# Expert tiles rounded to 64 rows: 192-row tiles with a half-array tail, and two nests of conditional tiles

## Chip, cores, metric

One core of one Trainium2 chip. The metric is the device time of one execution in microseconds (us). Profiles come from single executions; the times that are compared come from several executions of both kernels on the same chip.

## The reference, cut to what matters

Chunked attention (4 batches, 8 heads, 768 positions, head size 64) gives 3072 rows of 512. Each row goes to one of 8 experts, or stays with the expert of the row before it:

```python
fresh_e = int(np.argmax(logits[b, s]))
e = fresh_e if s == 0 or local_gate[b, s] < 0.5 else prev_e
h = np.maximum(x[b, s] @ w1[e], 0.0)        # w1[e]: 512 x 1024
out[b, s] = p[e] * (h @ w2[e])              # w2[e]: 1024 x 512
```

Everything is float32. With the fixed inputs the experts get 561, 195, 431, 505, 757, 256, 96 and 271 rows.

## The kernel before

The rows are scattered to DRAM in the order of their experts, and the second half of the kernel walks over *tiles*: 128 rows of one expert, gathered by GpSimd. Every expert is rounded up to whole tiles. 24 tiles exist for any input ("sure"); up to 7 more are conditional, in nested branches on a count that the chip works out. "Hidden" is the first matmul with ReLU, "product" the second.

```python
def product(ht, w2_sb, xs, past):
    y_ps = yps.tile([P, D], F32, name="y_ps")
    for m in range(FK):
        nc.tensor.matmul(y_ps, lhsT=ht[:, m], rhs=w2_sb[:, m], start=(m == 0), stop=(m == FK - 1))
    # ... scale by the probability on ScalarE, then an indirect store by GpSimd

def maybe_tiles(ctx, xts):
    n_tiles = nc.values_load(n_i, ...)
    for j in range(NTILE - SURE):
        i = SURE - EARLY + j
        ctx.enter_context(tc.If(n_tiles > i))
        w1_sb, w2_sb = weights(late, i, wa)           # 4 MB, pool of two buffers
        ht = hidden(xts[j % 2], w1_sb)
        if j + 1 < NTILE - SURE:
            rows_turned(late, i + 1, rest[:, j + 1], xt=xts[(j + 1) % 2])   # transposes of the next tile
        product(ht, w2_sb, rest[:, j], late[2][:, i:i + 1])
# ... the loop over sure tiles: weights from three buffers (pools wa, wa, wb);
#     maybe_tiles stands before sure tile BRANCH = SURE - 4, whose weights wait in wb
```

## Time and profile before

| | us |
|---|---|
| timed, median of 3 | 516.05 |
| span of the profiled execution | 540.6 |
| of it, up to the first product | 147.5 |
| of it, first product to the end of the last ("tile stage") | 386.9 |
| one tile, hidden to hidden | 14.45 |

The profiled execution was 25 us slower than the timed ones.

### The profile page before, as it was taken

The numbers are of one execution on the slowest core, as the hardware profiler recorded it, in microseconds if no ns is written. First come the engines' busy times: TensorE is split into PE (matmuls) and PEld (weight loads), VectorE is DVE, ScalarE is ACT, GpSimd is POOL, SyncE is SP. The second block draws the span as 40 slices with busy tenths as digits, with TensorE's granted clock in tenths as the row PEclk, the third lists the DMA queues.
The fourth block names the chain that finished last, engine by engine and source line by source line (L and its number), as shares of the span: only waits on it lengthen the run. The fifth ranks groups of instructions, "written<-read, shape, count | busy, mean of one in ns | idle before, by whom it ended". The sixth has DMA issues, their size and how long they took to land. (4 is left out here: it accounts for less than half of the span.)

```text
span 540.6 us, 9452 instructions
## 1 busy us (share of the span) xinstructions
PE 517.5 (96%) x3604; PEld 395.8 (73%) x3604; DVE 103.0 (19%) x394; ACT 112.5 (21%) x234; POOL 95.8 (18%) x141
## 2 busy tenths in 40 slices
PE   8997897889899999999999999999999999999995
PEld 6997786788776777777777777777777677777772
DVE  2464555635433000000000000000000100000000
ACT  4564445332211111011111110111011011111110
POOL 2002211530333211111111222221110100010000
PEclk9999989956999999999999999999999999999998
DMA  8977767896999998998989899999999985069700
GB/s 303 380 251 230 219 201 224 267 399 271 326 341 312 388 342 333 342 330 313 332 317 325 329 336 337 348 328 356 349 341 326 341 303 212 21 257 413 306 21 19
DMA packets 52760, 157.98 MB, mean 292 GB/s; under 512 B 7707, under 2 KB 11805, under 8 KB 52704
## 3 DMA queue, kind: packets, MB, share of 16 engines
q1 hardware_dynamic: 45696, 135.96, 70.5%
q0 software_dynamic: 6720, 20.78, 10.3%
q8 instruction: 32, 0.52, 0.4%
q10 hardware_dynamic: 288, 0.52, 0.3%
q14 instruction: 24, 0.20, 0.1%
HBM read 144.62 MB, written 13.40 MB: 292 GB/s over the span
## 5 line engine op out<-in xcount | busy, mean ns | idle before, releaser
L754 PE MATMUL y_ps<-w_sb,ht 128*128 128x512 f32 x416 | 183.0, 592 | 0.0
L743 PEld LDWEIGHTS h_ps<-gxt,w_sb 128*128 128x128 f32 x1408 | 160.7, 192 | 10.1 <-issue 10.1
L743 PE MATMUL h_ps<-gxt,w_sb 128*128 128x128 f32 x1408 | 161.3, 275 | 0.0
L754 PEld LDWEIGHTS y_ps<-w_sb,ht 128*128 128x128 f32 x416 | 76.9, 190 | 86.6 <-issue 85.9
L759 POOL DMA_INDIRECT out_dram<-y,to x27 | 27.3, 1010 | 235.6 <-ACT y L758 192.3
L681 DVE COPY gxt<-g_ps 128x512 f32<-128x512 f32 x22 | 15.2, 692 | 273.4 <-PE g_ps L678 269.7
L746 ACT ACTIVATE ht<-h_ps 128x512 f32<-128x512 f32 x54 | 32.2, 597 | 154.0 <-PE h_ps L743 105.2
L615 PE MATMUL o_ps<-vt,pt 128*96 128x65 f32 x512 | 57.2, 268 | 6.3 <-issue 6.2
L615 PEld LDWEIGHTS o_ps<-vt,pt 128*96 128x96 f32 x512 | 53.3, 183 | 10.7 <-issue 8.0
L758 ACT ACTIVATE y<-y_ps,xs 128x512 f32<-128x512 f32 x24 | 16.5, 687 | 161.8 <-PE y_ps L754 149.3
L463 POOL DMA_INDIRECT x_dram<-x,row x32 | 29.6, 925 | 102.9 <-DVE lt L385 66.2
L615 PEld LDWEIGHTS s_ps<-qt,kt 64*128 64x128 f32 x512 | 31.5, 196 | 6.6 <-issue 4.6
L615 PE MATMUL s_ps<-qt,kt 64*128 64x96 f32 x512 | 34.6, 286 | 0.6 <-ACT pt L345 0.4
L345 ACT ACTIVATE pt<-s_ps,mask_mid 128x256 f32<-128x256 f32 x72 | 28.1, 482 | 22.6 <-remote 9.8
L743 PE MATMUL h_ps<-held_xt,w_sb 128*128 128x128 f32 x256 | 29.3, 275 | 0.9 <-ACTq _compat.py:109 0.9
L743 PEld LDWEIGHTS h_ps<-held_xt,w_sb 128*128 128x128 f32 x256 | 28.9, 192 | 1.7 <-ACTq _compat.py:109 1.7
L355 DVE TENSOR_TENSOR x<-o_ps,rinvs 96x256 f32<-96x256 f32 x64 | 26.2, 417 | 1.2
L363 ACT COPY xt<-xt_ps 128x384 f32<-128x384 f32 x32 | 15.4, 482 | 42.1 <-PE xt_ps L615 32.4
L574 POOL DMA_INDIRECT xs<-x_dram,rows_late x19 | 18.3, 963 | 11.2 <-DMA x_dram<-x,row 5.7
L354 DVE RECIPROCAL rinvs<-o_ps 96x4 f32<-96x4 f32 x64 | 10.7, 172 | 48.0 <-PE o_ps L615 42.3
L615 PE MATMUL xt_ps<-ident,x 96*128 96x96 f32 x128 | 18.2, 270 | 0.5 <-ACT xt L363 0.5
L756 POOL TENSOR_TENSOR to<-xs,past_late 128x1 int32<-128x1 int32 x19 | 3.5, 187 | 77.4 <-DMA out_dram<-y,to 72.8
(163 smaller groups left out, 218.7 us busy)
## 6 DMA issues: line engine op xcount, KB each, us to landing
w_sb<-in_w_dram SPq DMA_DIRECT2D x216, 512.0 KB
vt<-in_v_dram SPq DMA_DIRECT2D x32, 260.0 KB
kt<-in_k_dram SPq DMA_DIRECT2D x30, 256.0 KB
qt<-in_q_dram SPq DMA_DIRECT2D x32, 192.0 KB
kt<-in_k_dram ACTq DMA_DIRECT2D x2, 256.0 KB
x_dram<-x,row POOLq DMA_INDIRECT x32, 6.0
out_dram<-y,to POOLq DMA_INDIRECT x27, 8.0
xs<-x_dram,rows_late POOLq DMA_INDIRECT x19, 6.6
```

The lines of the kernel that those rows point to most:

```text
L345: nc.scalar.activation(pt[:, :, :, c], st[:, :, :, c], ACT.Exp, bias=m[:, g:g + 1], scale=SCALE)
L355: nc.vector.tensor_tensor(x[:, 0:D].rearrange("p (a u d) -> p u a d", u=2, d=DH)[:, u], o_ps[:, :, 0:DH], rinv.to_broadcast([QB, HP, DH]), ...
L363: nc.scalar.copy(xt, xt_ps)
L463: ins = nc.gpsimd.indirect_dma_start(out=x_dram[:, :], out_offset=bass.IndirectOffsetOnAxis(ap=row[:, n:n + 1], axis=0), in_=x[0:QB, j + n ...
L574: ins = nc.gpsimd.indirect_dma_start(out=xs.bitcast(I32), out_offset=None, in_=x_dram[:, :], in_offset=bass.IndirectOffsetOnAxis(ap=rows[: ...
L615: return lambda *a, **k: tc.keep_in_program_order(f(*a, **k))
L681: nc.vector.tensor_copy(xt, g_ps)
L743: nc.tensor.matmul(h_ps[:, m], lhsT=w1_sb[:, kk, P * (g + m):P * (g + m) + P], rhs=xt[:, kk], start=(kk == 0), stop=(kk == DK - 1))
L746: nc.scalar.activation(ht[:, g:g + 4], h_ps, ACT.Relu)
L754: nc.tensor.matmul(y_ps, lhsT=ht[:, m], rhs=w2_sb[:, m], start=(m == 0), stop=(m == FK - 1))
L758: nc.scalar.activation(y, y_ps, ACT.Copy, scale=xs[:, D:D + 1])
L759: return nc.gpsimd.indirect_dma_start(out=out, out_offset=bass.IndirectOffsetOnAxis(ap=to, axis=0), in_=y, in_offset=None, bounds_check=NT ...
```

## The change

Its intent: to round experts up to 64 rows instead of 128. Where a rest of 64 would have cost a whole tile, a *wide* tile of 192 rows takes it along: hidden runs on 192 columns, and the last 64 rows' product puts the two halves of the output columns side by side on the two column halves of the array. There are now twelve sure tiles, a nest of up to 19 conditional ones, and a second nest of up to 8 wide ones. For these inputs 27 tiles become 5 early, 16 late and 3 wide.

```diff
-SURE = NT // P
-NTILE = SURE + E - 1
+UNIT = 64
+MORE = P + UNIT
+SURE = 12
+NTILE = 31
@@ plan_late
...
+        units = whole(total, "units", UNIT - 1, UNIT)
+        nc.vector.scalar_tensor_tensor(units, done, -2.0, units, ALU.mult, ALU.add)
+        pairs = whole(units, "pairs", 1, 2)
...
+        nc.vector.scalar_tensor_tensor(wide, pairs, 2.0, units, ALU.mult, ALU.is_gt)
+        nc.vector.scalar_tensor_tensor(wide, units, 2.0, wide, ALU.is_gt, ALU.mult)
...
+    def unit_product(ht, w2_sb, xs, past, y):
+        d = D // 2
+        y_ps = xps.tile([P, d], F32, name="yu_ps", tag="xps")
+        for m in range(FK):
+            for u in range(2):
+                h = slice(UNIT * u, UNIT * u + UNIT)
+                nc.tensor.matmul(y_ps[h], lhsT=ht[:, m, P:MORE], rhs=w2_sb[:, m, d * u:d * u + d],
+                                 start=(m == 0), stop=(m == FK - 1), tile_position=(0, UNIT * u))
...
+    def wide_tiles(ctx, n_wide):
+        for j in range(E):
+            ctx.enter_context(tc.If(n_wide > j))
+            if j + 1 < E:
+                wide_gathered(j + 1)
+            w1_sb, w2_sb = weights(wide, j, wa)
+            ht = hidden(wide_xt[j % 2], w1_sb, rows=MORE, ht=wide_ht[j % 2])
+            if j + 1 < E:
+                wide_turned(j + 1)
+            xs, xs_unit = wide_slots(j)
+            product(ht, w2_sb, xs, wide[2][:, j:j + 1])
+            unit_product(ht, w2_sb, xs_unit, unit[2][:, j:j + 1], wide_y[j % 2])
...
         if i == BRANCH:
-            maybe_tiles(held_xt[1:])
...
+            maybe_tiles(n_tiles)
+            wide_tiles(n_wide)
```

Left out: the gathers of conditional rows move into the first nest, two tiles ahead; for the wide tiles one tile ahead; the late plan gets two more parts.

More of the change, by code (lines that the diff above doesn't have):

```diff
@@ L42 @@
 BRANCH = SURE - 4
+RING = 4
 LOADS = 6
@@ L477, in totals, with plan @@
         return total
-    def plan(name, nt, sums):
+    def plan(name, nt, sums, unit=False):
         no = iota([P, nt, 1], [[1, nt], [0, 1]], 0, 0, f"no_{name}")
-        place = iota([P, nt, 1], [[P, nt], [0, 1]], 1, 1, f"place_{name}")
+        if unit:
+            place = one([P, nt, 1], F32, f"place_{name}")
+            for u in range(2):
+                nc.gpsimd.iota(place[UNIT * u:UNIT * u + UNIT], pattern=[[P, nt], [0, 1]], base=P + 1,
+                               channel_multiplier=1, allow_small_or_imprecise_dtypes=True)
+        else:
+            place = iota([P, nt, 1], [[P, nt], [0, 1]], 1, 1, f"place_{name}")
         table = one([1, nt], I32, f"table_{name}")
@@ L489, in all_tiles @@
             return a.rearrange("p (o e) -> p o e", o=1).to_broadcast([P, nt, n])
-        scratch = sm.tile([P, nt * PLAN], F32, name=f"scratch_{name}")
+        scratch = sm.tile([P, (NTILE - EARLY) * PLAN], F32, name="scratch")
         at, parts = 0, []
@@ L509, in plan @@
         nc.vector.tensor_tensor(is_past, place_at, last, op=ALU.is_gt)
-        nc.vector.tensor_scalar(past, is_past, float(FAR), None, ALU.mult)
+        if unit:
+            for u in range(2):
+                h = slice(UNIT * u, UNIT * u + UNIT)
+                nc.vector.tensor_scalar(past[h], is_past[h], 2.0 * FAR, float(u), ALU.mult, ALU.add)
+        else:
+            nc.vector.tensor_scalar(past, is_past, float(FAR), None, ALU.mult)
         nc.vector.tensor_tensor(place_at, place_at, last, op=ALU.min)
@@ L534, in plan_sums, with whole @@
         return sums
-    def tiles_of(total, name, more):
-        i = sm.tile([E, 1], I32, name=f"tiles_i_{name}")
-        nc.vector.tensor_scalar(i, total, float(more), None, ALU.add)
-        nc.vector.tensor_scalar(i, i, 7, None, ALU.logical_shift_right)
-        t = sm.tile([E, 1], F32, name=f"tiles_{name}")
+    def whole(a, name, more, size):
+        i = sm.tile([E, 1], I32, name=f"{name}_i")
+        nc.vector.tensor_scalar(i, a, float(more), None, ALU.add)
+        nc.vector.tensor_scalar(i, i, size.bit_length() - 1, None, ALU.logical_shift_right)
+        t = sm.tile([E, 1], F32, name=name)
         nc.vector.tensor_copy(t, i)
@@ L546, in plan_early @@
         total = totals("early", FORE)
-        full = tiles_of(total, "early", 0)
+        full = whole(total, "tiles_early", 0, P)
         yield
@@ L560, in plan_late @@
         total = totals("late", B)
-        tiles = tiles_of(total, "late", P - 1)
-        nc.vector.tensor_tensor(tiles, tiles, done, op=ALU.subtract)
-        sums = plan_sums("late", total, tiles, done)
-        n_i = once.tile([1, 1], I32, name="n_i")
-        nc.vector.tensor_copy(n_i, sums[0:1, E:E + 1])
-        return plan("late", NTILE - EARLY, sums), n_i
+        units = whole(total, "units", UNIT - 1, UNIT)
+        nc.vector.scalar_tensor_tensor(units, done, -2.0, units, ALU.mult, ALU.add)
+        pairs = whole(units, "pairs", 1, 2)
+        wide = one([E, 1], F32, "wide")
+        nc.vector.scalar_tensor_tensor(wide, pairs, 2.0, units, ALU.mult, ALU.is_gt)
+        nc.vector.scalar_tensor_tensor(wide, units, 2.0, wide, ALU.is_gt, ALU.mult)
+        tiles = one([E, 1], F32, "tiles_late")
+        nc.vector.scalar_tensor_tensor(tiles, wide, -2.0, pairs, ALU.mult, ALU.add)
+        before_wide = one([E, 1], F32, "before_wide")
+        nc.vector.tensor_tensor(before_wide, tiles, done, op=ALU.add)
+        n_i = once.tile([1, 2], I32, name="n_i")
+        sums = plan_sums("late", total, tiles, done)
+        nc.vector.tensor_copy(n_i[:, 0:1], sums[0:1, E:E + 1])
+        late = plan("late", NTILE - EARLY, sums)
+        sums = plan_sums("wide", total, wide, before_wide)
+        nc.vector.tensor_copy(n_i[:, 1:2], sums[0:1, E:E + 1])
+        return late, plan("wide", E, sums), plan("unit", E, sums, unit=True), n_i
     SP = mybir.EngineType.SP
@@ L680, in rows_turned, with unit_turned @@
             xt = hp.tile([P, DK, P], F32, name="gxt")
-        nc.vector.tensor_copy(xt, g_ps)
+        nc.vector.tensor_copy(xt[:, :, 0:P], g_ps)
         return xt, past[:, i:i + 1]
+    def unit_turned(xs, xt):
+        g_ps = xps.tile([P, DK, UNIT], F32, name="u_ps", tag="xps")
+        for kk in range(DK):
+            nc.tensor.transpose(g_ps[:, kk], xs[0:UNIT, P * kk:P * kk + P], identity=ident[:UNIT, :UNIT])
+        nc.vector.tensor_copy(xt[:, :, P:MORE], g_ps)
     def first_turned():
@@ L721, in everything @@
     flat = rinvs.rearrange("p n u a o -> p (n u a o)")
-    ok = sm.tile([P, (NTILE - EARLY) * PLAN], F32, name="scratch_late")[0:QB, 0:NB * H]
+    ok = sm.tile([P, (NTILE - EARLY) * PLAN], F32, name="scratch")[0:QB, 0:NB * H]
     nc.vector.tensor_scalar(ok, flat, 1.0 / SAFE, None, ALU.is_ge)
@@ L735, in everything, with hidden @@
     yps = ctx.enter_context(tc.tile_pool(name="yps", bufs=2, space=PSUM))
-    def hidden(xt, w1_sb, between={}):
-        ht = hp.tile([P, FK, P], F32, name="ht")
-        for g in range(0, FK, 4):
-            h_ps = hps.tile([P, 4, P], F32, name="h_ps")
-            for m in range(4):
+    def hidden(xt, w1_sb, between={}, rows=P, ht=None):
+        if ht is None:
+            ht = hp.tile([P, FK, P], F32, name="ht")
+        many = 512 // rows // 2 * 2
+        for g in range(0, FK, many):
+            h_ps = hps.tile([P, many, rows], F32, name="h_ps")
+            for m in range(many):
                 for kk in range(DK):
-                    nc.tensor.matmul(h_ps[:, m], lhsT=w1_sb[:, kk, P * (g + m):P * (g + m) + P], rhs=xt[:, kk],
-                                     start=(kk == 0), stop=(kk == DK - 1))
-                if m == 3:
-                    nc.scalar.activation(ht[:, g:g + 4], h_ps, ACT.Relu)
+                    nc.tensor.matmul(h_ps[:, m], lhsT=w1_sb[:, kk, P * (g + m):P * (g + m) + P],
+                                     rhs=xt[:, kk, 0:rows], start=(kk == 0), stop=(kk == DK - 1))
+                if m == many - 1:
+                    nc.scalar.activation(ht[:, g:g + many], h_ps, ACT.Relu)
                 for f in between.get(g + m, ()):
@@ L753, in product @@
         for m in range(FK):
-            nc.tensor.matmul(y_ps, lhsT=ht[:, m], rhs=w2_sb[:, m], start=(m == 0), stop=(m == FK - 1))
+            nc.tensor.matmul(y_ps, lhsT=ht[:, m, 0:P], rhs=w2_sb[:, m], start=(m == 0), stop=(m == FK - 1))
         to = hp.tile([P, 1], I32, name="to", bufs=4)
@@ L761, in product, with maybe_gathered, wide_slots, wide_gathered @@
             bounds_check=NT - 1, oob_is_err=False).ins
+    half_rows = out.rearrange("n (u d) -> (n u) d", u=2)
+    def unit_product(ht, w2_sb, xs, past, y):
+        d = D // 2
+        y_ps = xps.tile([P, d], F32, name="yu_ps", tag="xps")
+        for m in range(FK):
+            for u in range(2):
+                h = slice(UNIT * u, UNIT * u + UNIT)
+                nc.tensor.matmul(y_ps[h], lhsT=ht[:, m, P:MORE], rhs=w2_sb[:, m, d * u:d * u + d],
+                                 start=(m == 0), stop=(m == FK - 1), tile_position=(0, UNIT * u))
+        to = hp.tile([P, 1], I32, name="to", bufs=4)
+        token = xs[:, D + 1:XW].bitcast(I32)
+        nc.gpsimd.tensor_tensor(to, token, past, op=ALU.add)
+        nc.gpsimd.tensor_tensor(to, to, token, op=ALU.add)
+        nc.scalar.activation(y, y_ps, ACT.Copy, scale=xs[:, D:D + 1])
+        nc.gpsimd.indirect_dma_start(
+            out=half_rows, out_offset=bass.IndirectOffsetOnAxis(ap=to, axis=0), in_=y, in_offset=None,
+            bounds_check=2 * NT - 1, oob_is_err=False)
+    def maybe_gathered(j):
+        gathered(late, SURE - EARLY + j, range(B), rest[:, j % RING])
+    def wide_slots(j):
+        return rest[:, RING + 2 * (j % 2)], rest[:, RING + 2 * (j % 2) + 1]
+    def wide_gathered(j):
+        for t, xs in zip((wide, unit), wide_slots(j)):
+            gathered(t, j, range(B), xs)
+    def maybe_turned(j):
+        rows_turned(late, SURE - EARLY + j, rest[:, j % RING], xt=held_xt[1 + j % 2])
+    def wide_turned(j):
+        xs, xs_unit = wide_slots(j)
+        rows_turned(wide, j, xs, xt=wide_xt[j % 2])
+        unit_turned(xs_unit, wide_xt[j % 2])
     @with_exitstack
-    def maybe_tiles(ctx, xts):
-        n_tiles = nc.values_load(n_i, min_val=SURE - EARLY, max_val=NTILE - EARLY,
-                                 skip_runtime_bounds_check_because="a count of tiles")
+    def maybe_tiles(ctx, n_tiles):
+        last = NTILE - SURE - 1
         for j in range(NTILE - SURE):
@@ L769, in maybe_tiles @@
             ctx.enter_context(tc.If(n_tiles > i))
+            if j + 2 <= last:
+                maybe_gathered(j + 2)
             w1_sb, w2_sb = weights(late, i, wa)
-            ht = hidden(xts[j % 2], w1_sb)
-            if j + 1 < NTILE - SURE:
-                rows_turned(late, i + 1, rest[:, j + 1], xt=xts[(j + 1) % 2])
-            product(ht, w2_sb, rest[:, j], late[2][:, i:i + 1])
+            ht = hidden(held_xt[1 + j % 2], w1_sb)
+            if j < last:
+                maybe_turned(j + 1)
+            product(ht, w2_sb, rest[:, j % RING], late[2][:, i:i + 1])
+    @with_exitstack
+    def wide_tiles(ctx, n_wide):
[7 more added lines that the diff above has]
+                wide_turned(j + 1)
+            xs, xs_unit = wide_slots(j)
+            product(ht, w2_sb, xs, wide[2][:, j:j + 1])
+            unit_product(ht, w2_sb, xs_unit, unit[2][:, j:j + 1], wide_y[j % 2])
     pools = (wa, wa, wb)
@@ L791, in everything @@
         if i == 2:
-            late, n_i = plan_late(done)
+            late, wide, unit, n_i = plan_late(done)
+            rest = xp.tile([P, NQB, XW], F32, name="x")
+            wide_xt, wide_ht, wide_y = [], [], []
+            for _ in range(2):
+                flat = xp.tile([P, NQB, XW], F32, name="x").rearrange("p n w -> p (n w)")
+                at = 0
+                for parts, n in ((wide_xt, DK), (wide_ht, FK)):
+                    parts.append(flat[:, at:at + n * MORE].rearrange("p (n w) -> p n w", n=n))
+                    at += n * MORE
+                wide_y.append(flat[:, at:at + D // 2])
         if i == BRANCH:
-            maybe_tiles(held_xt[1:])
+            _, (n_tiles, n_wide) = nc.values_load_multi_w_load_instructions(
+                n_i, min_val=0, max_val=NTILE, skip_runtime_bounds_check_because="counts of tiles")
+            maybe_tiles(n_tiles)
+            wide_tiles(n_wide)
         if late is not None:
@@ L799, in everything @@
                 tile_w.append(weights(late, len(tile_w) - EARLY, pools[len(tile_w) % 3]))
-        if i == BRANCH - 9:
-            rest = xp.tile([P, NQB, XW], F32, name="x")
-        if BRANCH - 9 <= i < BRANCH - 9 + NTILE - SURE:
-            j = i - (BRANCH - 9)
+        if BRANCH - 4 <= i < BRANCH - 2:
             with tc.issue_after(stored):
-                gathered(late, SURE - EARLY + j, range(B), rest[:, j])
+                maybe_gathered(i - (BRANCH - 4))
+        if i == BRANCH - 2:
+            with tc.issue_after(stored):
+                wide_gathered(0)
         w1_sb, w2_sb = tile_w[i]
@@ L815, in everything @@
         if i + 1 == BRANCH:
-            rows_turned(late, SURE - EARLY, rest[:, 0], xt=held_xt[1])
+            maybe_turned(0)
+            wide_turned(0)
         stored = product(ht, w2_sb, tile_xs[i], past)
```

## The prediction

> **What bounds the kernel now.** I began with the page's busy shares and its slices, then went through the TensorE timeline tile by tile, because the slices say which engine is full but not what one tile costs.
>
> ```profile
> PE 517.5 (96%) x3604; PEld 395.8 (73%) x3604; DVE 103.0 (19%) x394; ACT 112.5 (21%) x234; POOL 95.8 (18%) x141
> ...
> PE   8997897889899999999999999999999999999995
> ...
> PEclk9999989956999999999999999999999999999998
> DMA  8977767896999998998989899999999985069700
> ...
> L759 POOL DMA_INDIRECT out_dram<-y,to x27 | 27.3, 1010 | 235.6 <-ACT y L758 192.3
> ```
>
> The reader is to see two stages. About 150 us are attention and routing; from then on TensorE has a 9 in every slice at the full clock, and the rest of the kernel is 27 expert tiles (27 stores). DMA is nearly as busy (8 or 9 until late), so I asked whether a tile ever waits for weights. The timeline of TensorE around the three conditional tiles:
>
> ```profile
> 432.81 7.31 PE L743 MATMUL h_ps<-held_xt,w_sb 128*128 128x128 f32 x64
> 439.96 7.03 PE L754 MATMUL y_ps<-w_sb,ht 128*128 128x512 f32 x16
> 446.83 0.60 PE L678 MATMUL g_ps<-ident,x 128*128 128x128 f32 x4
> 447.26 7.31 PE L743 MATMUL h_ps<-held_xt,w_sb 128*128 128x128 f32 x64
> ...
> 468.86 7.03 PE L754 MATMUL y_ps<-w_sb,ht 128*128 128x512 f32 x16
> 476.77 7.41 PE L743 MATMUL h_ps<-held_xt,w_sb 128*128 128x128 f32 x64 [0.87 <-ACTq _compat.py:109]
> ```
>
> It does not: hidden starts are 447.26 - 432.81 = 14.45 us apart, conditional or not, which is 7.15 us of hidden (64 instructions, 111.7 ns each), 6.87 us of product (16, 429.4 ns each) and 0.43 us of transposes. TensorE's own rate is the bound; entering a conditional costs nothing visible, and leaving the nest costs 0.87 us. The work is therefore tiles times 14.45 us. What leaving does to the weight queue is in the waits of the DMA queue:
>
> ```profile
> SPq L597 <- PEq _compat.py:109: 16.6, 1, 16.6
> ```
>
> After the nest the first weight load sat 16.6 us until TensorE itself had left the nest. Here nobody noticed, since the next tile's weights lay in the third buffer.
>
> [...] the logits matmuls, on four column strips, did eight instructions of 384 columns in about two instruction times,
>
> ```profile
> 105.03 0.85 PE L615 MATMUL lt_ps<-xt,wg 128*32 128x384 f32 x8 [0.64 <-issue]
> 105.82 2.40 PE L615 MATMUL s_ps<-qt,kt 64*128 64x96 f32 x32
> ```
>
> that is 0.79 us from start to start [...] The trace shows halved stretches in attention, and one after its last matmul (which began at 533.8): the clock row ends in an 8.
>
> **The change part by part.** The counts come from running the reference's routing on its fixed inputs: 561, 195, 431, 505, 757, 256, 96 and 271 rows. Rounded to 128 these are 5, 2, 4, 4, 6, 2, 1, 3 tiles: 27, as the trace has. The early plan covers five whole tiles (one each of experts 1, 2 and 4, two of expert 3, from the counts after two batches). Rounded to 64 and with those taken off, the remaining units are 9, 2, 5, 4, 10, 4, 2, 5. Odd and over two: experts 0, 2 and 7. So three wide tiles replace two ordinary ones each: 5 early + 16 late + 3 wide. With twelve sure, nine conditional tiles run in the first nest and three in the second.
>
> - Removed: six ordinary tiles, 6 x 14.45 = **86.7 us**.
> - Added, three wide tiles. Hidden: 64 instructions of 192 columns. [...] Product of the first 128 rows: 6.87. Its transposes 0.43[...]. Product of the last 64 rows: 8 slices x 2 halves x 2 passes = 32 instructions of 256 columns[...]. Sum 10.41 + 6.87 + 0.43 + 0.65 + 3.74 = 22.1, x 3 = **66.3 us**. A wide tile saves 28.9 - 22.1 = 6.8 us over its two.
> - Added, the passage between the nests. The second nest's first weights go to one of the same two buffers and, as in the wait above, can be asked for only once TensorE has left the first nest. Nothing else is ready for TensorE: the next sure tile stands after both nests in program order. How long that load takes is in the trace of before, just after its nest ended at 475.89: I summed the queue's packets by landing time, and the fourth 512 KB piece, which completes the first weight matrix, landed at 483.53. So **7.6 us** idle, the 0.87 of leaving included. (Leaving the second nest costs the 0.87 that is already in the time before.) The windows view of the same place:
>
> ```profile
> 475.89:476.77 0.88, 0.01 (x2) 0.01 (x1) 0.00 (x0) 0.69 (x1) 0.00 (x0) 1.00 0.00 0
> 476.02:483.53 7.51, 6.76 (x60) 6.76 (x61) 0.00 (x0) 1.25 (x2) 1.36 (x3) 1.00 0.79 293
> ```
>
>   (columns: length, busy of TensorE, weight loads, VectorE, ScalarE, GpSimd, clock, DMA share, GB/s; 293 GB/s x 7.51 us = 2.2 MB, the 2.1 MB matrix and a little more).
> - Added, the clock. [...]
> - Added before the nests: the turning of the first wide tile, 1.08, and a wait for the single transpose buffer. Before, the first conditional tile's turning made that tile take 15.47 us where 14.45 + 0.43 would do: 0.6. Together **1.7 us**.
> - Added in the late plan: three small sums on TensorE (the present three take 0.76 us) and about 30 VectorE instructions. VectorE was done with its plan 10 us before the next tile's hidden, so only the sums lie on the path: **0.6 us**.
> - Moved: gathers of conditional rows into the nest (needed a tile later), and weight transfers, 27 to 24 sets. Neither was on the path. Nine conditional tiles in a row with two buffers is new, but each matrix is asked for 21 us before it is needed and takes about 6.
>
> Net: 86.7 - 66.3 - 7.6 - 2.6 - 1.7 - 0.6 = 7.9 us. The timed runs are 24 us shorter than the profiled one; tiles cannot be much of that[...], so I take the same difference off 516.05: **508.1 us**, 1.5% faster.
>
> **Rivals.**
> 1. No wait between the nests: the load starts earlier, or arrives behind the last tile. Speaks for it: a free buffer exists, because its last real user ended a tile earlier. Against: exactly that was so before as well, and the load still waited 16.6 us. It would make 498 us, over 3% faster.
> 2. The column halves run one after another (their weight loads, two to each step, get in the way; the logits loaded each strip only twice). Each wide tile then takes 3.5 us more: 518 us, no gain. The logits speak against it.
> 3. GpSimd becomes the new wait. After a nest it holds until its last store has landed (before, it resumed at 484.3, 8.4 us after TensorE's end); then it gathers the second wide tile's rows, about 2 us of issue and 6.6 to land: ready at 17.3 us, while the transposes want them at 7.6 + 2.6 + 10.4 = 20.6. Three us of slack; if it fails, or if the gathers inside the first nest make each tile wait for rows just asked for (1 to 2 us for nine tiles), the time is 510 to 522.
>
> **Range and chances.** The six-tile term is firm to 1 us, the wide tiles to 1.5, the passage with its clock to 3. That gives 504.0 to 512.5. Faster by over 2% needs under 505.9, thus a passage shorter by 2 or 3 us, or rival 1: 0.24. Slower by over 2% needs rivals 2 and 3 together: 0.05. Within 2%: 0.71.
>
> **What would show it.** 24 stores to whole rows or 21 + 3 plus 3 to half rows; conditional tiles 14.45 us apart; wide hidden instructions 163 ns apart; half-row products of about 3.6 us; one idle stretch of TensorE of 7 to 8 us ended by a weight DMA, with a halved clock after it. If that idle stretch is missing or under 4 us, the prediction is wrong on the fast side; if half-row products take 7 us or conditional tiles over 15, on the slow side.

The forecast's sum came to 86.7 - 66.3 - 7.6 - 2.6 - 1.7 - 0.6 = 7.9 us, thus 508.1. Terms of it rested on figures that no trace or run here shows: how 10.41 (hidden), 0.65 (transposes) and 3.74 (half-row product) were got in the 22.1 us of a wide tile, and the whole item of 2.6 us for a slower clock after the idle stretch. These numbers are my forecast, not something measured; so is the 3.5 us of rival 2. That tiles have little part in the 24 us was not shown at that time either.

What the trace of before does show: product instructions are 429.4 ns apart, so a 384-column instruction would take 384/512 of that, 322 ns, and eight in a row 2.58 us (an estimate from the 429.4). The eight of the logits, on four column strips, took 0.79 us, with 0.35 us from the first four to the next four. The granted clock was 0.50 from 66.12 to 72.94 and from 110.49 to 130.97 us, both in attention, and again from 537.16, after the last matmul.

## The result

The change takes **538.35 us** (median of 4 runs, 537.8 to 541.17) against 515.81 before (4 runs): ratio 1.0448, 95% interval 1.041 to 1.0486. It is slower by 4.5%.

The page of the kernel after (PEclk is the clock that TensorE was granted, in tenths of full speed, over 40 slices of the span):

```profile
PE 490.3 (91%) x3474; PEld 375.9 (70%) x3474; DVE 109.5 (20%) x437; ACT 111.0 (21%) x234; POOL 97.3 (18%) x149
...
PE   8999999999999999999999999992493986989995
...
PEclk9999999999999999999999999997697897999998
```

TensorE is busy 27 us less than before, in part because this profile's attention stage was faster; but its row, solid before, has a hole from slice 28 on, and the clock falls with it. That is the second nest. Its timeline on TensorE (columns: start, length, instructions, idle before and what ended it; PEq is TensorE's sequencer, and `_compat.py:109` stands for the branch code that the builder puts in):

```profile
358.11 7.03 PE L791 MATMUL y_ps<-w_sb,ht 128*128 128x512 f32 x16
383.10 1.09 PE L707 MATMUL g_ps<-ident,x 128*128 128x128 f32 x4 [17.96 <-DMA x<-x_dram,rows_wide]
383.98 3.02 PE L780 MATMUL h_ps<-x,w_sb 128*128 128x192 f32 x12
...
395.88 7.03 PE L791 MATMUL y_ps<-w_sb,x 128*128 128x512 f32 x16
402.84 3.67 PE L809 MATMUL yu_ps<-w_sb,x 128*64 128x256 f32 x32
415.61 1.09 PE L707 MATMUL g_ps<-ident,x 128*128 128x128 f32 x4 [9.09 <-DMA x<-x_dram,rows_wide]
...
446.55 1.09 PE L707 MATMUL g_ps<-ident,x 128*128 128x128 f32 x4 [6.73 <-DMA x<-x_dram,rows_wide]
...
472.51 7.38 PE L780 MATMUL h_ps<-held_xt,w_sb 128*128 128x128 f32 x64 [1.85 <-PEq _compat.py:109]
```

Read the second line: the first work that TensorE does in a wide tile is four transposes (`g_ps`), and it stood 18 us for their rows. They are not this tile's rows, which were turned before the nests; they are those of the *next* wide tile. The source has these transposes after hidden; the built program has them ahead of it, at the head of every wide tile. The program's own listing of TensorE says the same (cut to matmuls; the profile counts each float32 matmul twice, and transposes once):

```
CompareAndBranch
g_ps<-ident,x 128x128 x4        # next wide tile's rows
h_ps<-x,w_sb 128x192 x6
u_ps<-ident,x 128x64 x4
h_ps<-x,w_sb 128x192 x26
y_ps<-w_sb,x 128x512 x8
yu_ps<-w_sb,x 64x256 x16
```

GpSimd asks for those rows inside the same tile, and after a nest it is late:

```profile
366.72 1.01 POOL L796 DMA_INDIRECT out_dram<-y,to  x1 [11.63 <-POOLq _compat.py:109]
376.09 0.97 POOL L603 DMA_INDIRECT x<-x_dram,rows_wide  x1 [8.35 <-issue]
...
407.84 0.98 POOL L816 DMA_INDIRECT out_dram<-x,to  x1 [2.86 <-ACT x L815]
409.12 0.98 POOL L603 DMA_INDIRECT x<-x_dram,rows_wide  x1 [0.31 <-issue]
```

TensorE was done with the first nest at 364.98. GpSimd's last store of that nest left at 366.7; the sequencer's records then show it waiting on the semaphores of its transfers until 373.1 and in one more record (INC_SWDGE_SEM, 1.7 us) until 374.9, and the gather left at 376.1. In the second wide tile there is no such wait, but the gather still stands behind the tile before's last store (409.1).

The second nest takes 107.5 us from the end of the first nest's last product (364.98) to the next sure tile's hidden (472.51). The windows view of its pieces (length, busy TensorE, weight loads, VectorE, ScalarE, GpSimd, clock, DMA share, GB/s):

```profile
364.98:383.10 18.12, 0.16 (x1) 0.03 (x1) 0.00 (x0) 0.69 (x1) 3.45 (x6) 0.60 0.94 356
383.10:406.43 23.33, 23.33 (x120) 17.56 (x120) 1.12 (x2) 2.65 (x5) 1.01 (x1) 0.94 0.58 219
406.43:415.61 9.18, 0.09 (x3) 0.03 (x1) 0.00 (x0) 0.47 (x1) 3.45 (x6) 0.68 0.80 298
415.61:439.74 24.13, 24.13 (x120) 18.35 (x120) 1.11 (x2) 2.65 (x5) 1.02 (x1) 0.91 0.03 12
439.74:446.55 6.81, 0.08 (x2) 0.03 (x1) 0.00 (x0) 0.47 (x1) 3.47 (x6) 0.80 0.31 76
```

Three idle stretches, 18.1 + 9.2 + 6.8 us. In each the granted clock falls to 0.50, 3.8, 3.3 and 4.1 us after TensorE's last product ended (at 368.75, 409.71 and 443.84), and stays there for the first 2.7, 4.3 and 4.1 us of the work after it. The wide tiles take 23.3 to 24.1 us instead of some 22.

### The profile page after: what moved, and what is told of

It is laid out like the page before. It is cut to its first block, busy times and chain, and to the rows that moved or that the text cites. A ratio compares the mean times of both kernels' runs of the same rounds, so it can differ in the third digit from the quotient of the medians. Undisturbed runs are those within 1.5% of the kernel's fastest.

```text
span 536.1 us, 9227 instructions
## 1 busy us (share of the span) xinstructions
PE 490.3 (91%) x3474; PEld 375.9 (70%) x3474; DVE 109.5 (20%) x437; ACT 111.0 (21%) x234; POOL 97.3 (18%) x149
## 3 DMA queue, kind: packets, MB, share of 16 engines
q0 software_dynamic: 6624, 20.77, 10.5%
## 5 line engine op out<-in xcount | busy, mean ns | idle before, releaser
L791 PE MATMUL y_ps<-w_sb,ht 128*128 128x512 f32 x320 | 141.1, 593 | 0.0
L791 PEld LDWEIGHTS y_ps<-w_sb,ht 128*128 128x128 f32 x320 | 59.2, 190 | 66.0 <-issue 65.2
L796 POOL DMA_INDIRECT out_dram<-y,to x24 | 24.1, 1006 | 298.0 <-ACT y L795 244.3
L780 PEld LDWEIGHTS h_ps<-gxt,w_sb 128*128 128x128 f32 x640 | 73.1, 192 | 4.3 <-issue 4.3
L780 PE MATMUL h_ps<-held_xt,w_sb 128*128 128x128 f32 x640 | 73.2, 275 | 1.9 <-PEq _compat.py:109 1.9
L780 PEld LDWEIGHTS h_ps<-held_xt,w_sb 128*128 128x128 f32 x640 | 72.3, 192 | 2.3 <-issue 2.3
L780 PE MATMUL h_ps<-gxt,w_sb 128*128 128x128 f32 x640 | 73.6, 276 | 0.0
L644 PE MATMUL o_ps<-vt,pt 128*96 128x65 f32 x512 | 49.2, 249 | 0.1
L644 PEld LDWEIGHTS o_ps<-vt,pt 128*96 128x96 f32 x512 | 46.2, 165 | 2.2 <-DVE x L358 0.6
L707 PE MATMUL g_ps<-ident,x 128*128 128x128 f32 x56 | 9.9, 307 | 33.8 <-DMA x<-x_dram,rows_wide 33.8
L780 PE MATMUL h_ps<-x,w_sb 128*128 128x192 f32 x192 | 36.7, 356 | 0.0
L780 PEld LDWEIGHTS h_ps<-x,w_sb 128*128 128x128 f32 x192 | 35.6, 213 | 0.2
L710 DVE COPY held_xt<-g_ps 128x512 f32<-128x512 f32 x12 | 8.3, 688 | 129.6 <-PE g_ps L707 129.6
L644 PEld LDWEIGHTS s_ps<-qt,kt 64*128 64x128 f32 x512 | 29.9, 188 | 6.8 <-issue 4.6
L644 PE MATMUL s_ps<-qt,kt 64*128 64x96 f32 x512 | 32.7, 277 | 0.4 <-ACT pt L348 0.4
```

What stands on the lines that cost most here:

```text
L644: return lambda *a, **k: tc.keep_in_program_order(f(*a, **k))
L707: nc.tensor.transpose(g_ps[:, kk], xs[:, P * kk:P * kk + P], identity=ident)
L710: nc.vector.tensor_copy(xt[:, :, 0:P], g_ps)
L780: nc.tensor.matmul(h_ps[:, m], lhsT=w1_sb[:, kk, P * (g + m):P * (g + m) + P], rhs=xt[:, kk, 0:rows], start=(kk == 0), stop=(kk == DK - 1))
L791: nc.tensor.matmul(y_ps, lhsT=ht[:, m, 0:P], rhs=w2_sb[:, m], start=(m == 0), stop=(m == FK - 1))
L796: return nc.gpsimd.indirect_dma_start(out=out, out_offset=bass.IndirectOffsetOnAxis(ap=to, axis=0), in_=y, in_offset=None, bounds_check=NT ...
```

## The experiments

The first theory: the loss is the order of the transposes together with late rows. The first four runs shared one chip, which was a restless one: the kernel before took 538 to 552 us on it, at a mean granted clock of 0.943 to 0.982 (0.997 or 0.998 on the quiet chip). Timed ratios of that job are weak (slow: four of the seven runs of before and one each of e1, e2 and e4, the profiled ones of e1 and e4 among them), and I read the tile stage in the traces. The last four shared a quiet chip (before: 516.15, 9 runs, 515.29 to 516.71).

| run | tile stage, us | timed median, us | ratio to before, 95% |
|---|---|---|---|
| before | 386.9 | 515.81 | 1 |
| the change | 407.7 | 538.35 | 1.045 (1.041 to 1.049) |
| e1_in_order | 378.3 | 538.36, restless | 0.993 (0.981 to 1.004) |
| e2_rows_earlier | 395.1 | 558.32, restless | 1.027 (1.006 to 1.048) |
| e3_no_wide | 393.1 | 554.45, restless | 1.025 (1.016 to 1.033) |
| e4_tile_between | 371.9 | 529.2, restless | 0.975 (0.963 to 0.986) |
| e5_unit_first | 368.1 | 497.96 | 0.965 (0.963 to 0.966) |
| e6_in_order_again | 379.1 | 508.91 | 0.986 (0.984 to 0.988) |
| e7_between_again | 371.6 | 500.83 | 0.970 (0.969 to 0.971) |
| e8_after_again | 407.0 | 539.29 | 1.046 (1.044 to 1.048) |

All gave correct results. On the quiet chip the tile stage carries the differences: against before -18.8, -7.8, -15.3 and +20.1 us in the traces, -18.2, -7.2, -15.3 and +23.1 in the medians (e5, e6, e7, e8; the profiled run of e8 was its fastest, 2.7 us under the median).

### e1_in_order: the order alone

`pinned` makes every call of a function a `tc.keep_in_program_order`.

```diff
             maybe_tiles(n_tiles)
+            nc.tensor.matmul, nc.tensor.transpose = pinned(matmul), pinned(transpose)
             wide_tiles(n_wide)
+            nc.tensor.matmul, nc.tensor.transpose = matmul, transpose
```

> The change with TensorE's order in the wide nest pinned to the source's: hidden, then the next wide tile's transposes, then the product. Theory (order): the 33.8 us in which TensorE waited for rows_wide come from the next tile's transposes standing ahead of this tile's hidden. Pinned, the rows (landing 17 to 18 us after the first nest, and about 9 us into the later wide tiles) have arrived when asked for, since hidden takes 10.5; what stays is the wait for the first weights, 7 to 8 us after the first nest[...]. 538.4 - 10 - 9.1 - 6.7 - 3.5 = about 509 us (506 to 513). Rival (GpSimd is late wherever the transposes stand): the wait moves to the end of hidden and the time stays over 525.

(The last term of the sum, 3.5: no source.)

Measured: tile stage 378.3 us, 29.4 less than the change's, and the waits for `rows_wide` on TensorE are gone. The timed ratio on that chip is unclear (0.981 to 1.004), so the same kernel ran again:

> The change with its wide nest in source order, once more. Its tile stage was 378.3 us against 386.9: a ratio of 0.982 to 0.985, the time that the prediction gave for the change itself. Rival as above: over 0.99.

Measured: 508.91 us, ratio 0.9857, against 539.29 for the change on the same chip:

> The change itself beside the others on one chip. Its tile stage was 407.7 us against 386.9: ratio 1.040 to 1.045, with 33 us of waits for rows_wide; if the restless attention stage carries the loss, the ratio falls well below that.

The change came out at 1.0459. Both ratios lie just above the ranges expected. So TensorE's order inside the second nest, by itself, is worth 30 us. The timeline of the pinned kernel (the quiet run; L644 is the line of `pinned`):

```profile
358.26 7.03 PE L791 MATMUL y_ps<-w_sb,ht 128*128 128x512 f32 x16
369.83 0.98 PE L644 MATMUL h_ps<-x,w_sb 128*128 128x192 f32 x2 [4.54 <-DMA w_sb<-in_w_dram]
...
374.46 12.08 PE L644 MATMUL h_ps<-x,w_sb 128*128 128x192 f32 x58 [0.76 <-DMA w_sb<-in_w_dram]
386.38 0.60 PE L644 MATMUL g_ps<-ident,x 128*128 128x128 f32 x4
...
394.37 3.67 PE L644 MATMUL yu_ps<-w_sb,x 128*64 128x256 f32 x32
397.97 10.67 PE L644 MATMUL h_ps<-x,w_sb 128*128 128x192 f32 x64
408.47 0.60 PE L644 MATMUL g_ps<-ident,x 128*128 128x128 f32 x4
```

The transposes now follow hidden without a wait, wide products are 22.10 and 22.09 us apart, and what ends the idle stretch after the first nest is the weight DMA, piece by piece. The rival (GpSimd late wherever the transposes stand) is refuted.

### e2_rows_earlier: the rows alone

```diff
-            if j + 1 < E:
-                wide_gathered(j + 1)
             ...
             unit_product(ht, w2_sb, xs_unit, unit[2][:, j:j + 1], wide_y[j % 2])
+            if j + 2 < E:
+                wide_gathered(j + 2)
@@ at sure tile BRANCH - 2
                 wide_gathered(0)
+                wide_gathered(1)
```

> The change with the wide tiles' rows gathered one wide tile earlier (the second's ahead of both nests, each later one's at the end of the tile before), TensorE's order left to the scheduler. Theory (order meets late rows): the same gain as by pinning, about 509 us (506 to 513), with no wait for rows_wide left and 7 to 8 us for the first weights. Rival (the wait after the first nest is the nest's own joining of engines, not the rows): 18 us of idle remain and the time is over 520.

The expected time was missed (about 509 us, which is a tile stage of some 380): the tile stage is 395.1, only 12.6 less than the change's. The traces show why: "at the end of the tile before" is immediately ahead of the head of the next tile, where the transposes stand. Only the second wide tile's rows, gathered before both nests, were really early.

```profile
397.87 0.63 PE L707 MATMUL g_ps<-ident,x 128*128 128x128 f32 x4 [0.69 <-PEq _compat.py:109]
...
401.38 12.52 PE L780 MATMUL h_ps<-x,w_sb 128*128 128x192 f32 x64 [2.49 <-DMA w_sb<-in_w_dram]
413.73 7.03 PE L791 MATMUL y_ps<-w_sb,x 128*128 128x512 f32 x16
...
429.36 1.08 PE L707 MATMUL g_ps<-ident,x 128*128 128x128 f32 x4 [4.99 <-DMA x<-x_dram,rows_wide]
434.95 0.66 PE L716 MATMUL u_ps<-ident,x 64*128 64x64 f32 x4 [4.51 <-DMA x<-x_dram,rows_unit]
```

For the passage the theory held: from the start of the first nest's last product (390.14) to the start of the first wide product it took 23.59 us, against 37.78 in the change, with the transposes still at the head and no wait for rows before them. So the rival (the nest's joining of engines holds TensorE 18 us) falls. For the later tiles the edit only moved the wait: 5.0 + 4.5 us here, and 2.6 + 3.6 in the third tile.

### e3_no_wide: everything but the wide tiles

```diff
+        nc.vector.tensor_scalar(wide, wide, 0.0, None, ALU.mult)
         tiles = one([E, 1], F32, "tiles_late")
```

> The change with the count of wide tiles multiplied by zero: 27 ordinary tiles, 15 of them conditional, and the second nest passed over. It measures all that the change adds outside of wide tiles. Theory (the loss lies inside the second nest): the time before plus about 1 us of extra turning, 1 of planning and 2 for leaving a second nest: 518 to 520 us. Rival (long conditional nests or the early part cost): over 524, with conditional tiles more than 14.45 us apart.

Measured: tile stage 393.1, 6.2 us over the kernel before, where 4 had been expected. Conditional tiles are 14.45 us apart, fifteen in a row, so the rival falls; the extra turning and planning cost 1.3; the other 4.9 are where the nests end:

```profile
474.76 7.03 PE L792 MATMUL y_ps<-w_sb,ht 128*128 128x512 f32 x16
485.99 9.01 PE L781 MATMUL h_ps<-held_xt,w_sb 128*128 128x128 f32 x64 [4.20 <-PEq _compat.py:109]
```

The sequencer's records for TensorE around it (start, ns):

```
475.633 3440 COMPARE_BRANCH     leaves the first nest; the last product still runs
481.988  196 COMPARE_BRANCH
482.243 3372 COMPARE_BRANCH     passes over the second nest; nothing runs
485.673   51 EVENT_SEMAPHORE
```

The branch that jumps out of, or over, a nest holds TensorE's sequencer for 3.3 to 4.0 us; the traces of before, of the change and of all experiments have it. Before, it took 3.72 us from 469.73, beside 6 us of queued product that ran until 475.89, and cost nothing.

The traces say more of it. All ten have such branches, 29 in all with the one near the end of each kernel, of 3.30 to 4.05 us. Inside each, a 16 KB packet on queue q8 (of kind "instruction" in the DMA view) begins 0.9 to 1.4 us after the branch, and the branch ends 1.3 to 1.5 us after that packet has landed; no branch of under 0.2 us has one that begins inside it. In before and the change, for instance, there are five such branches of 3.32 to 3.86 us; their packets begin 0.92 to 1.02 us after the branch and land 1.36 to 1.49 us before its end. In the two longest, of e4 and e7, another such packet was still under way. Why the branch takes so long was not shown; no run moved its target. The branch was new to me and gave the last improvement below.

### e4_tile_between and e7_between_again: the wait for weights

With rows and order mended, 9 us of waiting for the first weights remain after the first nest. Here the sure tile whose weights are held anyway stands between the nests, the three weight buffers are three pools, and of the sure tile after the nests the first matrix is asked for before the second nest and the other after it. Rows come earlier as in e2, and the order is pinned as in e1. The main part of the edit:

```diff
         if i == BRANCH:
             maybe_tiles(n_tiles)
-            wide_tiles(n_wide)
+            w, rest_of_w = weights_begun(late, BRANCH + 1 - EARLY, wa)
+            tile_w.append(w)
+            for f in rest_of_w[:DK]:
+                f()
+        if i == BRANCH + 1:
+            nc.tensor.matmul, nc.tensor.transpose = pinned(matmul), pinned(transpose)
+            wide_tiles(n_wide)
+            nc.tensor.matmul, nc.tensor.transpose = matmul, transpose
+            for f in rest_of_w[DK:]:
+                f()
```

> A version meant to beat both: rows one wide tile earlier, order pinned, and the sure tile whose weights are held stands between the two nests, so that the wide nest's first weights load beside it (three single weight buffers; of the sure tile after the nests the first matrix is asked for before the second nest, the other after it). Theory: on top of the 509 us of the two above, the wait for weights of about 8 us and its slow clock of about 2.5 go: 497 to 501 us. Rival (the two weight sets asked for together delay each other past the 15 us of that tile): 503 to 508.

(Beside its "about 2.5": in the pinned runs the 58 hidden instructions after the last wait took 11.4 us (e1) and 11.9 (e6), where 58 x 10.50/64 = 9.5 would do at full clock: 1.9 and 2.4 us more.)

> The version with the tile between the nests once more, in more rounds, as the chip of the first job had a slow and restless attention stage (the kernel before took 538 to 552 us there). From its own trace the tile stage is 371.9 us against 386.9 before, so 15 us less: a ratio of 0.970 to 0.973. Rival (some of that is given back in the attention stage): over 0.98.

Measured: tile stages of 371.9 and 371.6; timed on the quiet chip 500.83 us, ratio 0.970, both as expected. The first nest's exit costs 0.87 us again, with no wait for weights. What is left is at the second nest's exit:

```profile
442.70 3.67 PE L645 MATMUL yu_ps<-w_sb,x 128*64 128x256 f32 x32
448.80 6.44 PE L781 MATMUL h_ps<-held_xt,w_sb 128*128 128x128 f32 x41 [2.42 <-PEq _compat.py:109]
```

A 4.05 us branch began at 444.07, when only 2.2 us of half-row product were left, and a halved clock of 3.4 us followed (in e4, at the same place, hidden took 8.90 us instead of 7.31).

### e5_unit_first: work behind which the branch can hide

```diff
-            product(ht, w2_sb, xs, wide[2][:, j:j + 1])
             unit_product(ht, w2_sb, xs_unit, unit[2][:, j:j + 1], wide_y[j % 2])
+            product(ht, w2_sb, xs, wide[2][:, j:j + 1])
```

> The version with the tile between the nests, and in a wide tile the half-row product ahead of the full-row one. Theory (the branch out of a nest takes TensorE's sequencer 3.4 to 4.0 us in every trace, and is hidden only while work queued behind it lasts; before the exit of the second nest stand short instructions of 108 ns, while after a full-row product stand 6 us of work): the idle stretch at the second nest's exit falls from 2.8 to about 1.4 us and no slow clock window follows it; first product to last 371.9 - 3.5 = about 368.5 us. Rival (the exit waits for ScalarE or GpSimd to finish the tile): nothing changes.

(Beside its 108 ns: 32 of these instructions took 3.60 us in the pinned trace, 112 ns each.)

Measured: tile stage 368.1, 497.96 us, ratio 0.9646: faster than both kernels. The last wide tile and the exit:

```profile
435.69 3.67 PE L645 MATMUL yu_ps<-w_sb,x 128*64 128x256 f32 x32
439.30 7.13 PE L645 MATMUL y_ps<-w_sb,x 128*128 128x512 f32 x16
447.31 7.41 PE L781 MATMUL h_ps<-held_xt,w_sb 128*128 128x128 f32 x64 [0.87 <-ACTq _compat.py:109]
```

The branch (3.32 us from 439.32) ends long before the product does; the exit is 0.87 us as in the kernel before (1.4 had been expected); and the clock record is at full rate from 7.0 us until after the last product. The rival is refuted.

## Why the prediction was wrong

It said 508.1 us, within 2%; the change took 538.35. By its own steps:

- **Counts** (27 tiles become 21 and 3 wide): right.
- **Conditional tiles at 14.45 us**: right, nine and even fifteen in a row.
- **A wide tile, 22.1 us**: right. Pinned and at full clock, wide products are 22.10 and 22.09 apart: hidden 10.50 (predicted 10.41), half-row product 3.60 (3.74). What these two started from stands in no trace; the trace has 429.4 ns for a product instruction, and 192/512 of that is 161 ns and gives 10.3 us for hidden (an estimate), so nothing hangs on it.
- **Passage between the nests, 7.6 us, and the term of 2.6 for slow clock**: both were there in the pinned kernel, where hidden waits for its last weight piece until 9.3 us after the first nest (374.46 - 365.13) and the 58 remaining instructions take 11.9 us instead of 9.5, so 2.4 of slow clock. In the change itself the passage was 18.1 us, and the weights were not what came last.
- **Turning and plan, 1.7 + 0.6 us**: somewhat high. The tile after the plan took 0.67 us more and the tile of the first turning 1.0 more, but the tile ahead of the plan 0.6 less (a wait at 163.28 in the trace of before is gone): 1.1 net.
- **Exit of the second nest, "the 0.87 that is already in the time before"**: too small. It was 1.9 us, as short instructions stand ahead of its branch.
- **"Gathers ... Neither was on the path", and rival 3's slack of three us**: this is the step that failed. Rival 3 had nearly the right time for the rows, 17.3 us after the first nest; TensorE went on 18.1 us after it. In part that is luck: the 484.3 that it starts from is a later wait, and in the trace of before GpSimd was past the nest and computing at 479.9, 4.0 us after TensorE's end, while in the change it waited for its last store and gathered 11.1 us after. The place was wrong: it had the transposes wanting them at 20.6, after hidden, because the source has them there. They stand at the head of the tile, so TensorE waited 18.1 us where 7.6 had been expected, and again 9.2 and 6.8 us where no wait had been.

The terms that were missed, from the change's trace against the prediction: passage 18.1 - 7.6 = 10.5; waits ahead of the second and third wide tile 9.2 + 6.8 = 16.0; slow clock, wide tiles of 23.3, 24.1 and 24.0 against 22.1, so 5.2 - 2.6 = 2.6; exit 1.1. All but the exit belong to the failed step. Together they are 30.2 us, and 508.1 + 30.2 = 538.3. That this meets the timed figure so closely is luck: the tile stage was off by 28.7 (407.7 against 386.9 - 7.9 = 379.0), as turning and plan came out 1.2 too high. Pinning removes the first three almost wholly: 508.91 us measured.

The sign was in the lines that the prediction itself showed. In the kernel before, the conditional tiles' timeline reads transposes (446.83), hidden (447.26), product (454.41), and the transposes end just where hidden begins; for sure tiles it reads hidden, transposes, product. I took the transposes at 446.83 for the end of one tile. They were the head of the next, with rows gathered long before, so that it cost nothing there.

The trace shows that the builder put them ahead. Why it did so was not tested.

## What to carry to other kernels

Take the order of an engine's instructions from the trace or the built program, not from the source: an instruction that has been harmless at the head of a block can become the bound when its input is made in that same block (here 34 us of waits). When a nest of conditional tiles ends, every engine has its own lateness (here GpSimd about 11 us until its next gather, the weight queue 9 us until a full matrix, TensorE's branch 3.3 to 4.0 us); put work that needs none of these beside the exit, such as a tile whose weights and rows are already there, and long matmuls ahead of the branch. The idea of the change was sound: mended in order and place, it gave 3.5%.

## What else the traces show of the hardware

- Compare-and-branches that go on into the next conditional tile took 65 to 86 ns on TensorE's sequencer (before, the change), the one after a nest's exit 192 to 196 ns (before, the change, e3_no_wide), and those that leave or pass over a nest 3.3 to 4.05 us, also with nothing else running (3.37 us in e3_no_wide).
- In the tile stage of the change the clock was back at full rate 2.7 to 4.3 us after work began again; in the quiet pinned run after about 4.9 us (twice the 2.4 us lost there, an estimate). In the attention stage of the profile before, the clock was at 0.50 for 20.5 us (110.49 to 130.97), of which the profile counts TensorE busy for 20.3. Four transposes took 0.84 us there and 0.50 outside, so the record is not at fault. Why, no run here tests.
- With float32 and new weights at every step, 32 half-width instructions took 3.60 us, thus 112 ns each, where half of a 512-column instruction's 429.4 ns is 215 ns (an estimate): 1.9x from the two column halves.
- After the first nest of the change, GpSimd's next gather left 9.4 us after the store before it, 6.1 us of that in one wait on its last store and 1.7 us in INC_SWDGE_SEM.
